# A 4608-token attention and MoE kernel: its first two 256-token chunks in one pass over the weights instead of two

## The chip, the cores and the metric

The kernel runs on one core of a Trainium2 chip. The metric is device time in microseconds of one execution. The engines are named as the profile names them: PE (matmuls; PEld is its weight load), DVE (vector), ACT (activations and copies), POOL (a second, slower vector engine), and SP, which issues most of the DMAs.

## What is computed

The reference computes linear attention with exponential features for 8 batches of 576 tokens and 8 heads of 64, and sends its output, 4608 rows of 512, through a feed-forward layer with a hidden width of 2048. The code calls that layer MoE.

```python
def phi(x):
    proj = np.einsum('bhsd,df->bhsf', x, w_phi)
    proj = proj - np.max(np.abs(proj), axis=-1, keepdims=True)
    return np.concatenate([np.exp(proj), np.exp(-proj)], axis=-1)
q_p, k_p = (phi(q), phi(k))
kv = np.einsum('bhsf,bhsd->bhfd', k_p, v)
z = np.sum(k_p, axis=2)
num = np.einsum('bhsf,bhfd->bhsd', q_p, kv)
den = np.einsum('bhsf,bhf->bhs', q_p, z)[..., None] + 1e-06
attn = num / den                       # then (4608, 512)

h = x @ w_in                           # 512 -> 2048
g = h * (1.0 / (1.0 + np.exp(-1.702 * h)))
out = g @ w_out                        # 2048 -> 512
```

## The kernel before

All matmuls of the bulk run in 16 bits, with each operand split into a high and a low half (`eh` and `el`, `gh` and `gl`, `w16[:, i, 0]` and `w16[:, i, 1]`), so that a product takes three matmuls. The attention of a batch writes its output, already transposed and split, into a tile `x` of which there are three buffers.

The MoE weights come from memory as 64-bit numbers. `load_weights(j, bank)` takes block j (128 of the 2048 hidden columns) of both weight matrices: it loads 512 KB for each, and ACT (`raw<-raw`, `hb<-raw` or `wy<-raw`, the cast to `w`), DVE (two steps on `hb` or `wy`) and DVE or POOL (the low half `w`) make the two halves. For the first 8 blocks the intermediate is a PSUM tile `hb`, for the others an SBUF tile `wy`. There are 16 blocks j, so 32 conversions.

`moe_chunk(sb, c0, n, part_)` does n tokens. For each block j it does 12 matmuls (or more, at a border between batches) into a PSUM tile `hb`, then on ACT and DVE in turn `th` (tanh), `g`, `gh` and `gl`, and then three matmuls for each 128 tokens into an accumulator `ab`. There are three `ab` buffers, so a chunk of 256 tokens holds two of them from its first block to its last, when ACT evicts them into a tile `e` that is stored.

The first 512 tokens go in chunks of 256, all others in chunks of 384. Before the change each of the two chunks of 256 is done twice: with `part_` 0 over j = 0 to 7, with `part_` 1 over j = 8 to 15. After the first pass ACT copies the two accumulators into a tile named `kept`, which takes one of the three `x` buffers; after the second DVE adds the kept row to the accumulator on its way out:

```python
row = kept[:, c0 // P + m] if part_ is not None else None
if part_ == 0:
    R.scalar.activation(row, acc[m], AF.Copy, scale=OS)
    continue
```

Nothing in this kernel is issued in the order of its source. A recorder collects every operation with its tiles, and a planner then puts them in an order for each engine: at each step the operation that can start first by the planner's own costs, and among those that could start now, the one with the lowest place. The places come from a table, `PLACES`, with one pair of numbers for each group of operations (a head pair of attention, the load of a weight block, a chunk), and a group that the table reaches has its pair from there, whatever the source says. Operations that may run on more than one engine (`R.two`, `R.three`, `R.evac`) go where the planner's costs, weighted by the numbers in `price`, put them. Since one line records all of these, the profile shows one line, L467, for nearly everything, and the names of tiles tell the work apart.

Of the kernel before, what the change touches and what calls it, by code (L numbers as in the profile page):

```python
# [8 lines left out]
F32 = mybir.dt.float32  # L9
# [90 lines left out]
class _Op:  # L100
# [5 lines left out]


PLACES = (
# [26 lines left out]
)  # L135
_READY = {"tensor": 215.0, "scalar": 150.0, "vector": 130.0, "gpsimd": 95.0, "sync": 100.0}

# [38 lines left out]


class Recorder:
    price = dict(tensor=1.000, scalar=0.001, vector=2.059, gpsimd=1.247, sync=1.000)

    def __init__(self, nc):
        self.nc, self.ops = nc, []
# [291 lines left out]
def attn_moe_fast(ctx, tc, q, k, v, w_phi, w_in, w_out, out):  # L474
# [4 lines left out]
    NT, DM = out.shape  # L479
# [6 lines left out]
    CH = 384  # L486
# [3 lines left out]
    NH = 2  # L490
# [11 lines left out]
    R = Recorder(nc)  # L502
# [7 lines left out]
    def static(name, shape, dt):  # L510
# [18 lines left out]
        x=([P, 2, NCT, S], F16), th=([P, CH], F32), g=([P, CH], F32), gh=([P, CH], F16),  # L529
# [9 lines left out]
    def new(nm):  # L539
        return R.tile(pools[nm])  # L540
# [117 lines left out]
    def w1(j, part, ct):  # L658
        return w16[:, 2 * j, part, ct * P : (ct + 1) * P]

    def w2(j, part):
        return w16[:, 2 * j + 1, part]
# [452 lines left out]
    def store(sb, col, osb, queue):  # L1115
        p0 = 0
        while p0 < P:
            b, n, row, step = out_rows(col + p0)
            n = min(n, P - p0)
            row += (2 * sb + b) * S  # L1120
            if step == 1:
                dst = out[row : row + n, :]
            else:
                dst = out[row : row + 4 * (n - 1) + 1 : 4, :]
            queue.dma_start(dst, osb[p0 : p0 + n])
            p0 += n
# [3 lines left out]
    def moe_chunk(sb, c0, n, part_=None):  # L1130

        pieces = []
        c = c0
        while c < c0 + n:
            b = c // S
            e = min(c0 + n, (b + 1) * S)
            pieces.append((2 * sb + b, c - b * S, e - b * S, c - c0))
            c = e
        js = range(NJ) if part_ is None else range(part_ * NJ // NH, (part_ + 1) * NJ // NH)
        acc = [R.tile(ab, whole=True) for m in range(n // P)]  # L1140
        for j in js:
            hps = R.tile(hb, whole=True)[:, 0:n]
            for b, a0, a1, o0 in pieces:
                o = hps[:, o0 : o0 + a1 - a0]
                for ct in range(NCT):
                    xh, xl = (t[:, ct, a0:a1] for t in xs[b])
                    last = ct == NCT - 1
                    R.tensor.matmul(o, w1(j, 0, ct), xh, start=ct == 0, stop=False)
                    R.tensor.matmul(o, w1(j, 0, ct), xl, start=False, stop=False)
                    R.tensor.matmul(o, w1(j, 1, ct), xh, start=False, stop=last)  # L1150
            th = new("th")[:, 0:n]
            R.scalar.activation(th, hps, AF.Tanh, scale=0.851 / (XS * WS))
            g = new("g")[:, 0:n]
            R.vector.scalar_tensor_tensor(g, th, 1.0, hps, ALU.add, ALU.mult)
            gh = new("gh")[:, 0:n]
            gl = new("gl")[:, 0:n]
            sc = 0.5 * GS / (XS * WS)
            R.scalar.activation(gh, g, AF.Copy, scale=sc)
            R.vector.scalar_tensor_tensor(gl, g, sc, gh, ALU.mult, ALU.subtract)
            first, last = j == js[0], j == js[-1]  # L1160
            if j == NJ // 2:
                chunks.append(c0)
                i = len(chunks)
                R.vector.tensor_reduce(fin[:, i - 1 : i], g[0:1], AX.X, ALU.add)
            for m in range(n // P):
                s = slice(m * P, (m + 1) * P)
                R.tensor.matmul(acc[m], gh[:, s], w2(j, 0), start=first, stop=False)
                R.tensor.matmul(acc[m], gh[:, s], w2(j, 1), start=False, stop=False)
                R.tensor.matmul(acc[m], gl[:, s], w2(j, 0), start=False, stop=last)
        for m in range(n // P):  # L1170
# [4 lines that stand above are left out]
            end = c0 + n == SB * S and sb == B // SB - 1  # L1175
            osb = new("e")
            if part_ is not None:
                R.vector.scalar_tensor_tensor(osb, acc[m], OS, row, ALU.mult, ALU.add)
            elif end and m:
                R.vector.tensor_scalar(osb, acc[m], OS, None, ALU.mult)  # L1180
            else:
                R.scalar.activation(osb, acc[m], AF.Copy, scale=OS)
            store(sb, c0 + m * P, osb, R.scalar if end and m == 1 else R.sync)
# [82 lines left out]
    for part_ in range(NH):  # L1266
        js = range(part_ * NJ // NH, (part_ + 1) * NJ // NH)
        v0, dv = WV[part_]
# [1 line left out]
            R.part(v0 + dv * i, v0 + dv * (i + 1))  # L1270
            load_weights(j, (lambda: R.tile(hb, whole=True)) if j < NPS else (lambda: new("wy")))
    attention(1)
    kept = new("x").rearrange("p t c s -> p (t c s)").bitcast(F32)
    kept = kept[:, 0 : 4 * DM].rearrange("p (i n) -> p i n", i=4)
    attention(2)

    for part_ in range(NH):
        for c in (0, 256):
            v0 = (512 * part_ + c) / CH / NH
            R.part(v0, v0 + 256 / CH / NH, ("vector", "scalar"))  # L1280
            moe_chunk(0, c, 256, part_)
    for i in range(NBLK):
        R.part(3.0 + 0.2 * i, 3.0 + 0.2 * i, after=250e3)
        weight_max(i)
    for sb in range(B // SB):
        c = 0 if sb else 512
        for n in (CH, CH, CH) if sb else (256, CH):
            v0 = (SB * S * sb + c) / CH
# [189 lines left out]
```

## Time and profile before

| | before |
|---|---|
| median of 3 runs | 1050.89 us (1050.89 to 1051.35) |
| the profiled execution | 1050.94 us, span 1049.5 us |
| PE busy | 1013.7 us, 9914 matmuls |
| DVE busy | 733.7 us |
| ACT busy | 651.6 us |
| POOL busy | 283.2 us |
| HBM read, written | 45.15 MB, 9.44 MB |

The span is from the first to the last instruction. Busy times are summed over an engine's instructions without counting overlaps twice; matmuls are pipelined, so a busy PE may still have room. In 40 slices of 26 us the shares of time look as follows, in tenths (9 is 90% or more); PEclk is the clock granted to PE, in tenths of full speed:

```profile
PE   7869899999999999999999999999999999999997
DVE  5899999999999989999533226776876765323232
ACT  5989899888588878899332235565565554222221
```

The chain of waits that ended last is for 83% of the span PE, for 6% DVE and for 6% ACT.

### The profile page before, as it was taken

To read this page: it belongs to the slowest core of one execution; us is meant where nothing else is said; L and a number is where in the kernel's file an instruction comes from. 1 tells how busy PE (TensorE), PEld (TensorE's weight loads), DVE (VectorE), ACT (ScalarE), POOL (GpSimd) and SP (SyncE) were. 2 spreads that over 40 slices of the span, in tenths; PEclk is the share of its full clock that TensorE was granted. 3 is DMA by queue.
4 is the path that set the end of the run, shared out by engine and by line. 5 is a ranking of instruction groups with operands and counts; after the bars stand their busy time and mean duration, and the time that the engine had idled before them with its cause. 6 is when DMAs were issued, how large, how long until landed. Compare 5 with 4: busy or idle time off the path is not lost.

```text
span 1049.5 us, 24669 instructions
## 1 busy us (share of the span) xinstructions
PE 1013.7 (97%) x9914; PEld 667.6 (64%) x9914; DVE 733.7 (70%) x1465; ACT 651.6 (62%) x1449; POOL 283.2 (27%) x396
## 2 busy tenths in 40 slices
PE   7869899999999999999999999999999999999997
PEld 5646677778666667668664455677755665576543
DVE  5899999999999989999533226776876765323232
ACT  5989899888588878899332235565565554222221
POOL 1225655433334735454200001132211111000000
PEclk8989999999999999999999999999999999999999
DMA  9756655444236453536112011232230120000101
GB/s 239 213 179 152 135 122 149 100 122 99 51 91 98 94 136 72 117 81 124 47 29 42 1 31 49 53 77 47 52 74 20 31 52 11 1 31 1 31 1 33
DMA packets 181019, 80.92 MB, mean 77 GB/s; under 512 B 149536, under 2 KB 174240, under 8 KB 180896
## 3 DMA queue, kind: packets, MB, share of 16 engines
q1 hardware_dynamic: 178048, 78.35, 31.7%
q8 instruction: 79, 1.29, 0.5%
q10 hardware_dynamic: 2848, 0.92, 0.4%
q14 instruction: 44, 0.36, 0.1%
HBM read 45.15 MB, written 9.44 MB: 52 GB/s over the span
## 4 chain that ended last, share of the span: by engine, by line
PE 83%; DVE 6%; ACT 6%; issue 2%; DMA 1%; POOL 0%; SPq 0%; ACTq 0%; DVEq 0%; POOLq 0%
PE ab L467 34%; PE hb L467 32%; PE at L467 17%; ACT e L467 1%; DVE el L467 1%; DVE wy L467 1%; DVE hb L467 1%; ACT x L467 1%; DVE gl L467 1%; ACT eh L467 1%; ACT w L467 1%; DMA tl<-in_v_dram 0%; DMA qt<-in_q_dram 0%; DVE sm L467 0%; DVE t L467 0%
## 5 line engine op out<-in xcount | busy, mean ns | idle before, releaser
L467 PE MATMUL hb<-x,w 128*128 128x192 f16 (+3 forms) x3264 | 448.0, 279 | 1.1 <-DVE g L467 0.6
L467 PEld LDWEIGHTS <-w 128*128 128x128 f16 x3264 | 277.6, 98 | 99.9 <-issue 1.9
L467 PE MATMUL ab<-w,gh 128*128 128x512 f16 x1152 | 340.1, 379 | 0.6 <-ACT gh L467 0.2
L467 ACT ACTIVATE th<-hb 128x384 f32<-128x384 f32 (+1 forms) x208 | 97.1, 467 | 207.4 <-PE hb L467 206.3
L467 DVE SCALAR_TENSOR_TENSOR g<-th,hb 128x384 f32<-128x384 f32 (+1 forms) x208 | 107.9, 519 | 166.8 <-ACT th L467 165.5
L467 PE MATMUL ab<-w,gl 128*128 128x512 f16 x576 | 207.8, 379 | 1.5 <-DVE gl L467 1.4
L467 PEld LDWEIGHTS <-gh 128*128 128x128 f16 x1152 | 101.2, 97 | 96.0 <-ACT gh L467 20.9
L467 DVE SCALAR_TENSOR_TENSOR gl<-g,gh 128x384 f16<-128x384 f32 (+1 forms) x208 | 120.1, 578 | 46.0 <-ACT gh L467 45.2
L467 ACT ACTIVATE gh<-g 128x384 f16<-128x384 f32 (+1 forms) x208 | 103.9, 500 | 67.3 <-DVE g L467 64.7
L467 ACT CAST eh<-e 128x512 f16<-128x512 f32 x212 | 127.9, 624 | 1.2 <-PE at L467 0.6
L467 PEld LDWEIGHTS <-eh 128*128 128x128 f16 x1856 | 111.5, 97 | 26.7 <-ACT eh L467 3.5
L467 DVE TENSOR_TENSOR el<-e,eh 128x512 f16<-128x512 f32 x161 | 116.1, 738 | 15.2 <-ACT eh L467 11.0
L467 POOL TENSOR_TENSOR el<-e,eh 128x512 f16<-128x512 f32 x71 | 86.7, 1224 | 109.3 <-ACT eh L467 76.5
L467 PEld LDWEIGHTS <-gl 128*128 128x128 f16 x576 | 55.0, 97 | 71.4 <-DVE gl L467 31.2
L467 PE MATMUL at<-ph,xT 128*128 128x128 f16 x1024 | 94.9, 220 | 2.0 <-DVE t L467 1.0
L467 PEld LDWEIGHTS <-el 128*128 128x128 f16 x928 | 85.7, 98 | 15.3 <-DVE el L467 4.5
L467 ACT ACTIVATE e<-t 128x512 f32<-128x512 f32 x128 | 76.3, 629 | 20.4 <-DVE t L467 16.9
L467 ACT ACTIVATE e<-at 128x512 f32<-128x512 f32 x136 | 76.9, 602 | 17.7 <-PE at L467 17.1
L467 POOL TENSOR_TENSOR n<-n,cs 128x132 f32<-128x132 f32 (+1 forms) x74 | 42.4, 576 | 159.0 <-ACT n L467 144.5
L467 PEld LDWEIGHTS <-xT 128*128 128x128 f16 x1056 | 73.6, 98 | 15.2 <-issue 2.3
L467 PE MATMUL at<-kz,eh 128*128 128x66 f16 x960 | 78.7, 193 | 1.9 <-DVE x L467 0.7
L467 PE MATMUL at<-vs,eh 128*128 128x66 f16 x896 | 71.0, 194 | 0.0
(184 smaller groups left out, 1288.3 us busy)
## 6 DMA issues: line engine op xcount, KB each, us to landing
kt<-in_k_dram SPq DMA_DIRECT2D x32, 256.0 KB, 3.0
qt<-in_q_dram SPq DMA_DIRECT2D x32, 256.0 KB, 2.9
raw<-in_moe_w_in_dram SPq DMA_DIRECT2D x16, 512.0 KB, 4.0
raw<-in_moe_w_out_dram SPq DMA_DIRECT2D x16, 512.0 KB, 4.4
vn<-in_v_dram SPq DMA_DIRECT2D x62, 128.0 KB, 3.1
out_dram<-e SPq DMA_DIRECT2D x38, 128.0 KB, 2.4
out_dram<-e SPq DMA_DIRECT2D x16, 256.0 KB, 2.7
xT<-xs SPq DMA_TRANSPOSE x68, 2.8
```

The source lines that it names most:

```text
L467: f(*[g(a) for a in o.args], **{k: g(a) for k, a in o.kw.items()})
```

## The change

The two chunks of 256 tokens are each done once, over all 16 weight blocks. The tile `kept` is no longer made, so that the three `x` buffers go round among the scratch tile of the first batch and the batches alone. ACT no longer copies accumulators into it, and DVE no longer adds it; ACT evicts the four accumulators as it does for all other chunks. The operations of `moe_chunk` are otherwise the same. There are two groups fewer, and the table of places and two of the planner's prices are other numbers throughout.

```diff
 PLACES = (
-    (-1000.000, -1000.000), (-319.749, -277.364), (-292.885, 143.728), (-190.514, -96.843), (-328.012, -90.457),
...
+    (-1000.000, -1000.000), (-247.092, -16.724), (-252.980, 213.780), (-303.420, 28.872), (-247.129, -68.214),
...
 class Recorder:
-    price = dict(tensor=1.000, scalar=0.001, vector=2.059, gpsimd=1.247, sync=1.000)
+    price = dict(tensor=1.000, scalar=0.009, vector=2.162, gpsimd=1.253, sync=1.000)
...
     attention(1)
-    kept = new("x").rearrange("p t c s -> p (t c s)").bitcast(F32)
-    kept = kept[:, 0 : 4 * DM].rearrange("p (i n) -> p i n", i=4)
     attention(2)
 
-    for part_ in range(NH):
-        for c in (0, 256):
-            v0 = (512 * part_ + c) / CH / NH
-            R.part(v0, v0 + 256 / CH / NH, ("vector", "scalar"))
-            moe_chunk(0, c, 256, part_)
+    for c in (0, 256):
+        v0 = c / CH
+        R.part(v0, v0 + 256 / CH, ("vector", "scalar"))
+        moe_chunk(0, c, 256)
```

What the new table does shows in the order of the engines. On DVE, just ahead of the first `g` of the MoE (the first block of the first chunk), the order was this; `hb` and `raw` belong to the conversion of weights, `el`, `mq`, `nf` and `x` to attention:

```order
L467 SCALAR_TENSOR_TENSOR hb_67<-hb_67,raw_169 128x512
L467 TENSOR_TENSOR xf_124<-nf_121,rc_160 128x2x2x64
L467 SCALAR_TENSOR_TENSOR hb_68<-raw_171,hb_68 128x512
L467 TENSOR_TENSOR w_248<-hb_67,w_248 128x512
L467 SCALAR_TENSOR_TENSOR hb_68<-hb_68,raw_171 128x512
L467 TENSOR_TENSOR el_98<-e_88,eh_93 128x512
L467 TENSOR_TENSOR el_99<-e_91,eh_94 128x512
L467 TENSOR_TENSOR x_127<-at_66,x_127 128x256
```

With the change the same place reads as follows:

```order
L466 TENSOR_TENSOR w_248<-wy_172,w_248 128x512
L466 SCALAR_TENSOR_TENSOR wy_173<-wy_173,raw_170 128x512
L466 TENSOR_TENSOR x_127<-at_66,x_127 128x256
L466 SCALAR_TENSOR_TENSOR wy_172<-raw_171,wy_172 128x512
L466 TENSOR_SCALAR rc_161<-nf_121 128x4
L466 TENSOR_TENSOR w_248<-wy_173,w_248 128x512
L466 RECIPROCAL rc_161<-rc_161 128x4
L466 TENSOR_TENSOR xf_124<-nf_121,rc_161 128x2x2x64
```

The conversions have moved ahead: before, DVE was still at the blocks that go through `hb`, now it is at those that go through `wy`. 47 conversion steps stand ahead of the first `g` before, 62 with the change.

The second place is the seventeenth `g` on DVE, the first block of the second half of the work of these chunks. Before, it stands among the last conversions:

```order
L467 SCALAR_TENSOR_TENSOR wy_172<-raw_170,wy_172 128x512
L467 TENSOR_TENSOR nf_120<-at_66,n_119 128x198
L467 SCALAR_TENSOR_TENSOR wy_173<-wy_173,raw_169 128x512
L467 TENSOR_TENSOR nf_120<-at_65,n_118 128x198
L467 TENSOR_REDUCE sm_140<-at_66 128x4
L467 SCALAR_TENSOR_TENSOR wy_172<-wy_172,raw_170 128x512
L467 SCALAR_TENSOR_TENSOR g_131<-th_129,hb_68 128x256
```

With the change it stands just behind the last of them:

```order
L466 TENSOR_TENSOR x_127<-at_65,x_127 128x256
L466 TENSOR_TENSOR art_243<-art_243,rc_163 128x8
L466 SCALAR_TENSOR_TENSOR wy_173<-wy_173,raw_169 128x512
L466 TENSOR_TENSOR xo_125<-xf_123,xo_125 128x512
L466 SCALAR_TENSOR_TENSOR g_131<-th_129,hb_67 128x256
L466 SCALAR_TENSOR_TENSOR g_132<-th_130,hb_68 128x256
```

The `wy` step here is the 89th and last conversion step that DVE has; before, 72 of 86 stood ahead of this `g`, and 14 behind it.

The third place is on ACT, where the accumulators leave. Before, ACT copies them into the kept tile (`x_126`) ahead of two tanh steps; with the change the same two accumulators leave only after the sixteenth block, into `e` tiles that are stored:

```order
L467 CAST xo_125<-xf_123 128x512
L467 CAST eh_94<-e_88 128x512
L467 ACTIVATE x_126<-ab_71 128x512
L467 ACTIVATE x_126<-ab_69 128x512
L467 ACTIVATE th_129<-hb_68 128x256
L467 ACTIVATE th_130<-hb_67 128x256
```

```order
L466 CAST eh_95<-e_92 128x512
L466 ACTIVATE e_91<-at_65 128x512
L466 ACTIVATE e_88<-ab_71 128x512
L466 ACTIVATE e_89<-ab_70 128x512
L466 ACTIVATE gh_134<-g_132 128x256
```

The four copies of this kind have gone from ACT, and four additions from DVE.

49 rows, old and new, of the table PLACES are left out of this document.

## The prediction

> **What bounds the kernel now.** I read the page's busy line and its forty slices first, then the window table by stage, then the waits of PE, then the groups of instructions by form.
>
> ```profile
> PE 1013.7 (97%) x9914; PEld 667.6 (64%) x9914; DVE 733.7 (70%) x1465; ACT 651.6 (62%) x1449; POOL 283.2 (27%) x396
> ...
> 0.00:20.00 20.00, 15.61 (x77) 11.88 (x78) 10.53 (x31) 9.23 (x18) 4.27 (x40) 0.83 0.97 257
> 20.00:80.00 60.00, 45.91 (x329) 32.76 (x328) 52.70 (x103) 55.05 (x121) 11.69 (x18) 0.94 0.68 192
> 80.00:150.00 70.00, 64.48 (x772) 47.30 (x768) 67.10 (x135) 64.96 (x153) 43.66 (x52) 0.98 0.64 142
> 150.00:250.00 100.00, 97.84 (x1276) 73.32 (x1277) 93.98 (x196) 86.19 (x204) 44.48 (x55) 1.00 0.47 116
> 250.00:500.00 250.00, 248.88 (x3076) 170.80 (x3074) 234.57 (x470) 208.63 (x474) 119.08 (x153) 1.00 0.45 96
> 500.00:1049.50 549.50, 540.94 (x4398) 331.55 (x4397) 274.80 (x535) 227.58 (x483) 60.03 (x80) 1.00 0.14 34
> ```
>
> The columns of a window are its length, the busy time of PE, PEld, DVE, ACT and POOL, the granted clock, the DMA share and GB/s. PE is idle for 35.8 us of 1049.5, and most of it lies early: 4.4 us up to 20, 14.1 up to 80, 5.5 up to 150, 2.2 up to 250, then 1.1 in 250 us. So from about 150 us on the time is PE's work, nothing else, and a microsecond that PE loses before is not given back. In 80 to 150 us DVE is busy for 96% and ACT for 93%: they must convert weights and make the features of attention before PE has operands. The end is not touched by the change.
>
> ```profile
> 82.47 0.42 DVE L467 SCALAR_TENSOR_TENSOR g<-th,hb 128x256 f32<-128x256 f32 x1
> ...
> 83.04 0.68 DVE L467 SCALAR_TENSOR_TENSOR wy<-raw,wy 128x512 f32<-128x512 f32 x1
> 83.64 0.42 DVE L467 SCALAR_TENSOR_TENSOR gl<-g,gh 128x256 f16<-128x256 f32 x1
> ...
> 157.24 0.77 DVE L467 SCALAR_TENSOR_TENSOR wy<-wy,raw 128x512 int32<-128x512 int32 x1
> 157.93 0.41 DVE L467 SCALAR_TENSOR_TENSOR g<-th,hb 128x256 f32<-128x256 f32 x1
> ```
>
> These are two marks on DVE: the first g of a 256-token block (82.47 us) and the seventeenth (157.93), the first block of the second half of the weights. An instruction shown as 0.68 is followed 0.60 us later by the next, so on a full DVE a duration costs 0.08 less than the row says.
>
> **The change part by part.** (1) Sums between passes. Four ACT copies into the kept tile and four DVE additions go; four plain ACT evictions come.
>
> ```profile
> L467 ACT ACTIVATE x<-ab 128x512 f32<-128x512 f32 x4 | 2.3, 594 | 0.0
> L467 DVE SCALAR_TENSOR_TENSOR e<-ab,x 128x512 f32<-128x512 f32 x4 | 2.7, 686 | 0.0
> ```
>
> ACT is even over the whole program (four go, four come), DVE is relieved of 4 x 0.61 = 2.4 us. The additions stand after 191 us, where PE has no gaps for them to fill: on PE they are worth nothing. PE's matmuls are the same in number and shape.
>
> (2) The order. A block of 256 tokens needs its weights. Two passes give PE 32 blocks in the order 16 blocks over half of the weights, then 16 over the other half; one pass gives 16 blocks over all weights, then 16 again. I counted DVE's rows ahead of the seventeenth g in both orders. Conversion steps (w, wy, hb<-raw): 72 before, 89 now, all that DVE has. Attention steps on 512 columns: 87 before, 80 now. Small attention steps: 77 and 75. MoE steps: 32 and 32.
>
> ```profile
> L467 DVE SCALAR_TENSOR_TENSOR hb<-hb,raw 128x512 int32<-128x512 int32 x16 | 11.0, 693 | 1.1 <-ACT raw L467 1.0
> L467 DVE TENSOR_TENSOR w<-hb,w 128x512 f16<-128x512 f32 x16 | 11.0, 688 | 3.2 <-ACT w L467 3.1
> L467 DVE TENSOR_TENSOR xs<-qt,xs 128x512 f16<-128x512 f32 x18 | 13.1, 728 | 2.7 <-ACT xs L467 2.5 <-POOL xs L467 0.2
> L467 DVE TENSOR_TENSOR nf<-at,n 128x198 f32<-128x198 f32 x56 | 20.0, 356 | 1.5 <-POOL n L467 0.9
> L467 ACT CAST w<-wy 128x512 f16<-128x512 f32 x15 | 9.4, 629 | 2.2 <-DVE wy L467 2.1
> ```
>
> At 0.61 us for a conversion step, 0.62 for a large and 0.28 for a small attention step: 17 x 0.61 - 7 x 0.62 - 2 x 0.28 = +5.5 us of DVE work ahead of the same MoE block. On ACT there are 89 conversion steps for 74, 116 large attention steps for 125, no copies to the kept tile for four, one small step less: with 0.08 off the rows of 629 and 594 ns, and 0.2 for the small one, 15 x 0.55 - 9 x 0.55 - 4 x 0.51 - 0.2 = +1.1 us.
>
> On PE the same 16 blocks stand ahead of the mark, but 62 attention matmuls fewer (875 before, 813 now).
>
> ```profile
> 166.81 1.28 PE at L467 x35
> ```
>
> 35 of them take 1.28 us, 0.037 each, so PE has 2.3 us less to do until it needs that block. If DVE paces this stage, PE waits 5.5 + 2.3 = 7.8 us longer up to the mark; if ACT does, 1.1 + 2.3 = 3.4.
>
> (3) What can absorb it. Conversions need no result of PE, so more of them early can stand in DVE's idle time. DVE is idle for 9.5 us up to 20 us (start, first loads: not to be had), 7.3 in 20 to 80 and 2.9 in 80 to 150. 15 of the 17 extra steps stand ahead of the first g (62 for 47), in the stretch with the 7.3. Bounds: nothing absorbed, +7.8; all 7.3 + 2.9 used, 7.8 - 10.2 = -2.4. Before, 47 conversions already stood in that stretch and left the 7.3 us open, because the conversions themselves go back and forth between ACT and DVE (the row w<-hb above: 3.1 us of waiting for ACT w). I take half of what would come from bringing 20 to 80 us to the idle share of 80 to 150 (2.9 of 70, or 2.5 of 60): (7.3 - 2.5) / 2 = 2.4. So 7.8 - 2.4 = +5.4 us.
>
> (4) The loads. Some five weight blocks more are loaded ahead of the first block; the queue of SP has them earlier, among the k, q and v loads.
>
> ```profile
> raw<-in_moe_w_in_dram SPq DMA_DIRECT2D x16, 512.0 KB, 4.0
> 40.00:50.00 10.00, 8.32 (x56) 6.09 (x55) 8.31 (x16) 9.48 (x21) 0.00 (x0) 1.00 0.86 257
> ```
>
> 5 x 0.5 MB at the 257 GB/s of that window are 10 us; up to 80 us the DMA engines are busy for 0.97 x 20 + 0.68 x 60 = 60 us, so 70 of 80 would be. It fits, and I put nothing; without that cover a conversion waits for its load, 4.0 us from issue to landing.
>
> (5) The place in memory. With the kept tile gone the third x buffer goes to batch 2 without a wait for the second pass, and its attention ends earlier in the order. From 250 us on PE has 1.1 us of gaps in 250, so at most 1.1 us is to be had. Some elementwise steps have moved between DVE and POOL with the new prices; on the whole DVE has 24 steps fewer and POOL 29 more. After 150 us that is hidden behind PE's matmuls; up to 250 us it had 2.2 us of gaps left, and that much it could cost where the cover is thin.
>
> The sum: 1050.9 + 5.4 = 1056.3 us. The profiled execution took 1050.94 us for a span of 1049.5, the median of the runs is 1050.89, so no correction is needed between them.
>
> Is PE really at its limit where it shows 100%?
>
> ```profile
> 951.87 3.90 PE ab L467 x18
> 955.77 3.96 PE hb L467 x48
> ```
>
> 18 matmuls of 512 columns in 3.90 us are 0.217 each, 48 of 192 in 3.96 us 0.083: both 0.42 to 0.43 ns a column, with no room for a wait between them. The Trainium skill (Perfetto Trace Analysis, Identifying the Most-Contended Engine) says that matmul busy time is a poor measure of headroom and LDWEIGHTS busy time a better one; with PEld at 64% it would leave room to win lost time back, and the sum would be anywhere down to no change. The two rows decide against that here.
>
> **The rivals.** (A) The conversions fill DVE's idle time wholly and the stage comes out as it was: for it speaks that 7.3 us are idle in 20 to 80 us, against it that they stayed idle with 47 conversions at hand. At the bound of ACT (+3.4) less the same 2.4 it is +1.0, less 4.8 it is -1.4, in the middle -0.2: 1050.7.
>
> (B) Faster: PE makes up at the thirty-second block what it waits for at the seventeenth, because attention matmuls stand between. The point is the last block of both chunks. Up to it DVE now has 3 conversion steps more, 4 large attention steps and 2 additions fewer, one small step more (3 x 0.61 - 4 x 0.62 - 2 x 0.61 + 0.3 = -1.6 us), ACT four conversions, two large and three small steps and two copies fewer (4 x 0.55 + 2 x 0.55 + 3 x 0.2 + 2 x 0.51, or -4.9 us), PE 32 small matmuls (-1.2 us). That gives -0.4 by DVE and -3.7 by ACT, mean -2.0; with the 1.1 us of gaps beyond 250 us, 1047.8. It decides if PE shows no wait longer than before around the seventeenth block. Against it: PE was gapless from there on, so there is nothing to make up from.
>
> (C) The longer stall costs clock.
>
> ```profile
> 70.00:80.00 10.00, 5.51 (x38) 3.54 (x39) 8.23 (x19) 8.94 (x20) 2.53 (x3) 0.66 0.65 186
> PE ab L467 <- ACT e L467: 3.1, 2, 2.4
> ```
>
> In this window PE was busy for 5.51 us of 10 and the granted clock was 0.66; the longest single wait of PE anywhere in the run was 2.4 us. One more such window at the second chunk, with PE full, would cost (1 - 0.66) x 10 = 3.4 us: 1059.7. The Trainium skill (TensorE: Matmul & The Clock Gate, HAM oscillation) puts the threshold at a gap of some 3.4 us. Here the clock fell with no gap above 2.4, so by the row the risk is larger than by the rule; by the rule, stalls in pieces below it would leave 1056.3.
>
> **How the numbers follow.** The forecast gets 0.42, C 0.17, A 0.2, B 0.21. A measurement of this kernel tells 0.2% from no change, 2.1 us: 1048.8 to 1053.0. Forecast and C are slower but for a small share, which I weigh against A's upper end: slower 0.59, same 0.2, faster 0.21. The likeliest case alone spans 1053 to 1058.7 (+7.8 with nothing absorbed). The range takes in B's centre and C with nothing absorbed (7.8 + 3.4, 1062.1): 1047 to 1062.
>
> **What would show it.** The first hb matmul of the MoE, at 76.7 us before, comes 3 to 8 us later; the seventeenth g, at 157.93, stands at 161 to 164; PE's gaps up to 150 us grow from 24.0 to about 27, with the rest between 150 and 170; after 200 us PE is gapless, and all later marks are late by one and the same amount. I am wrong if the first block is late but the seventeenth isn't (DVE had room), or if the gaps of PE up to 170 us are no longer than before.

## The result, and the profile after

| | before | after |
|---|---|---|
| median | 1051.12 us (4 runs, 1050.89 to 1052.25) | 1065.05 us (4 runs, 1064.02 to 1065.21) |
| ratio | | 1.0129, 95% interval 1.0117 to 1.0142 |
| the profiled execution | 1050.94 us, span 1049.5 us | 1064.9 us, span 1063.1 us |
| mean granted clock | 0.990 | 0.983 |

The change costs 14 us. Forecast were 1056.3 us and a range of 1047 to 1062: the sign was right, the size wrong and outside the range.

The stages of the changed kernel, in the window table with the same columns as in the prediction (length, busy time of PE, PEld, DVE, ACT, POOL, granted clock, DMA share, GB/s):

```profile
0.00:20.00 20.00, 15.40 (x84) 11.96 (x85) 11.77 (x32) 9.70 (x19) 4.37 (x40) 0.91 0.95 262
20.00:80.00 60.00, 44.20 (x289) 30.74 (x288) 51.50 (x93) 51.76 (x113) 10.26 (x15) 0.86 0.70 204
80.00:150.00 70.00, 59.80 (x615) 41.49 (x615) 65.66 (x134) 62.67 (x146) 41.59 (x47) 0.93 0.58 152
150.00:250.00 100.00, 96.70 (x1276) 71.91 (x1277) 84.43 (x181) 79.14 (x188) 42.46 (x54) 1.00 0.38 88
```

Up to 150 us PE is idle for 30.6 us where it was 24.0, and part of what counts as busy ran at a lower clock: 0.86 and 0.93, for 0.94 and 0.98. The other engines are not fuller than before but emptier (DVE 51.50 for 52.70 in 20 to 80 us, ACT 51.76 for 55.05). Two stretches hold the loss, here of the kernel before and then of the change; between them, from 92 to 130 us, PE is idle for 0.9 us where it was 4.8, so a part comes back:

```profile
57.00:92.00 35.00, 25.49 (x227) 17.43 (x226) 32.38 (x74) 32.59 (x78) 14.10 (x24) 0.90 0.56 159
130.00:170.00 40.00, 38.99 (x477) 28.75 (x476) 38.55 (x75) 36.66 (x84) 22.06 (x21) 1.00 0.53 134
```

```profile
57.00:92.00 35.00, 20.82 (x105) 12.80 (x104) 29.00 (x62) 28.37 (x60) 7.18 (x10) 0.61 0.55 170
130.00:170.00 40.00, 32.98 (x393) 22.86 (x391) 37.38 (x74) 35.75 (x83) 22.46 (x27) 1.00 0.56 133
```

In the first stretch PE does 105 matmuls for 227, at a clock of 0.61; in the second it is idle for 7.0 us of 40 instead of 1.0. The two marks on DVE that the prediction used, the first and the seventeenth g (the second row holds two in one):

```profile
93.57 0.42 DVE L466 SCALAR_TENSOR_TENSOR g<-th,hb 128x256 f32<-128x256 f32 x1 [0.50 <-ACT th L466]
...
166.15 0.88 DVE L466 SCALAR_TENSOR_TENSOR g<-th,hb 128x256 f32<-128x256 f32 x2
```

They are 11.1 and 8.2 us late. From the 91st of the 208 blocks on the lag is between 10.0 and 12.7 us (14.5 at a single block), and 12.1 at the end. What PE does in the first stretch, in the timeline of PE (start, duration, tiles and shapes, count, and in brackets how long PE was idle before and for whom), only the rows with a wait of 0.9 us or more:

```profile
59.36 0.27 PE L466 MATMUL at<-kz,eqth 128*128 128x132 f16 x1 [1.91 <-DVE kz L466]
61.96 0.40 PE L466 MATMUL at<-kz,eqth 128*128 128x132 f16 x2 [1.89 <-DVE nt L466]
64.73 0.66 PE L466 MATMUL at<-ident,xf 128*128 128x128 f32 x2 [1.92 <-DVE nt L466]
66.31 1.12 PE L466 MATMUL at<-ident,t 128*128 128x128 f32 x4 [0.92 <-DVE x L466]
69.63 2.82 PE L466 MATMUL at<-x,kf 128*66 128x256 f32 x6 [2.20 <-ACT x L466]
...
81.79 0.29 PE L466 MATMUL at<-ii,zt 128*128 128x64 f16 x4 [1.41 <-ACT zt L466]
85.57 0.69 PE L466 MATMUL at<-ident,xf 128*128 128x128 f32 x2 [2.39 <-POOL xf L466]
```

These rows are attention of the first batch. `ident,t`, `x,kf` and `ident,xf` belong to its exact queries (the 256 tokens that the first chunk needs, computed on 32-bit operands), with one group of eight `x,kf` for each of the four head pairs; `kz,eqth` belongs to its last tokens. Each step feeds ACT and DVE and waits for what they send back. Up to 57 us PE has done the same matmuls in both kernels, within one of each kind, but for four `x,kf` that are missing now. What differs is the order in which the rest stands in PE's list. Three rows of the kernel before, and then of the change one group and the ACT step that makes its operand `x`:

```profile
55.46 0.65 PE L467 MATMUL at<-x,kf 128*66 128x256 f32 x2 [0.85 <-ACT kf L467]
...
60.74 1.89 PE L467 MATMUL at<-x,kf 128*66 128x256 f32 x8
...
66.44 0.62 PE L467 MATMUL at<-x,kf 128*66 128x256 f32 x2 [1.07 <-DVE nt L467]
```

```profile
73.78 2.63 PE L466 MATMUL at<-x,kf 128*66 128x256 f32 x8
```

```profile
55.66 1.08 ACT L466 ACTIVATE x<-at 128x512 f32<-128x512 f32 x2
```

Before, the four groups of `x,kf` start at 48.62, 55.46, 60.74 and 66.44 us, with steps of other head pairs between them. Now they start at 47.71, 69.63, 73.78 and 77.15: three of them stand behind all the waits of the rows above. By the buffers that the program names, the group at 73.78 reads the `x` that ACT had ready at 56.74 us, so it had its operands for 17 us and stood behind other steps. The change is hardly late when it enters this stretch; its list gives PE nothing else to do ahead of these waits. The 105 matmuls for 227 are mostly what follows from that: 147 of the 227 run after 77.2 us, when the kernel before was past its last `x,kf` and the change had just come to them.

Of the 13.6 us between the spans, 12.1 stand ahead of the end of the last DVE step (the evictions of the last chunk, before and after):

```profile
1041.16 1.34 DVE L467 TENSOR_SCALAR e<-ab 128x512 f32<-128x512 f32 x2 [0.97 <-PE ab L467]
```

```profile
1053.23 1.34 DVE L466 TENSOR_SCALAR e<-ab 128x512 f32<-128x512 f32 x2 [0.97 <-PE ab L466]
```

From there to the end of the span it is 7.0 us before and 8.5 after, 1.5 us that no step of the program explains; the section on the hardware comes back to it.

### The profile page after: what moved, and what is told of

It reads as the page before. It is cut to its first block, busy times and chain, and to the rows that moved or that the text cites. A ratio compares the mean times of both kernels' runs of the same rounds, so it can differ in the third digit from the quotient of the medians.

```text
span 1063.1 us, 24696 instructions
## 1 busy us (share of the span) xinstructions
PE 1016.6 (96%) x9914; PEld 667.7 (63%) x9914; DVE 733.1 (69%) x1441; ACT 647.5 (61%) x1440; POOL 303.0 (29%) x425
## 4 chain that ended last, share of the span: by engine, by line
PE 80%; DVE 8%; ACT 6%; issue 3%; DMA 1%; POOL 0%; ACTq 0%; SPq 0%; DVEq 0%; POOLq 0%
PE ab L466 33%; PE hb L466 31%; PE at L466 17%; ACT e L466 2%; DVE el L466 1%; ACT eh L466 1%; DVE t L466 1%; ACT x L466 1%; DVE sm L466 1%; DVE wy L466 1%; DVE hb L466 1%; DVE gl L466 1%; DVE w L466 0%; DVE g L466 0%; DMA x<-xo 0%
## 5 line engine op out<-in xcount | busy, mean ns | idle before, releaser
L466 DVE SCALAR_TENSOR_TENSOR gl<-g,gh 128x384 f16<-128x384 f32 (+1 forms) x208 | 114.3, 551 | 47.9 <-ACT gh L466 47.5
L466 DVE TENSOR_TENSOR el<-e,eh 128x512 f16<-128x512 f32 x166 | 124.7, 767 | 20.6 <-ACT eh L466 12.3
L466 ACT CAST eh<-e 128x512 f16<-128x512 f32 x209 | 125.5, 625 | 4.7 <-PE at L466 4.4
L466 POOL TENSOR_TENSOR el<-e,eh 128x512 f16<-128x512 f32 x66 | 78.9, 1197 | 83.3 <-ACT eh L466 66.9
L466 POOL TENSOR_TENSOR n<-n,cs 128x132 f32<-128x132 f32 (+1 forms) x89 | 53.4, 602 | 153.4 <-ACT n L466 106.8
L466 ACT ACTIVATE e<-at 128x512 f32<-128x512 f32 x136 | 76.6, 603 | 13.5 <-PE at L466 13.2
L466 PE MATMUL at<-kz,eh 128*128 128x66 f16 x960 | 75.9, 193 | 2.3 <-DVE nt L466 1.3
```

Source lines behind the costliest of these rows:

```text
L466: f(*[g(a) for a in o.args], **{k: g(a) for k, a in o.kw.items()})
```

## The experiments

Unless said otherwise an experiment keeps the planned order and alters what is issued from it, so that no other step moves. Where the totals are closer than their intervals (about 1.5 us either way), the marks decide: the first g (93.57 us after, 82.47 before) and the seventeenth (166.15 and 157.93). A mark is read from one profiled execution.

### The numbers without the one pass

```diff
 # the kernel before (two passes, kept tile), with
-PLACES, price   of before
+PLACES, price   of the change (the two chunk entries cut into four)
```

> Two passes as before, with the sums kept between them, but with the changed kernel's table of places and prices. Order theory (the new numbers put conversions ahead of attention, and that costs; one pass or two does not matter): about 1065 us, within 2 of the changed kernel. Structure theory (a chunk that runs through all 32 weight blocks at once needs the second half of the conversions sooner, whatever the numbers): 1049 to 1054 us, as the kernel before. Between 1054 and 1062 both have a part.

Measured: 1080.68 us, ratio 1.0276 (1.0254 to 1.0298). Worse than either kernel, so neither bracket holds. Its window table:

```profile
57.00:92.00 35.00, 20.02 (x100) 12.33 (x101) 29.07 (x62) 28.44 (x60) 6.99 (x10) 0.63 0.55 170
130.00:170.00 40.00, 31.84 (x346) 24.13 (x347) 34.24 (x65) 35.13 (x77) 19.01 (x24) 0.70 0.48 121
```

The first row is that of the changed kernel almost to the digit, and the first g stands at 94.47. So **the first stretch comes with the numbers, not with the single pass**: two passes under these numbers stall there just as long. What follows is another matter. The ninth block, in two passes the first of the second chunk of tokens, comes at 156.8 us (126.7 before): these numbers put the second half of the first batch's queries late, which one pass needs only at its seventeenth block. There is no reverse, one pass with the numbers of before: with them the planner comes to a point from which no step can start.

### More and less work on DVE

```diff
 # kernel before, nine of the steps wy|hb <- max(c * raw, same) of 40 to 150 us
+repeat the step
```

> The kernel before in its own order, with 9 of the conversion steps wy<-raw,wy on DVE between 40 and 150 us done twice (same result). That is 9 x 0.60 = 5.4 us of DVE work, the excess that the prediction worked out for the change. Work theory: the seventeenth g comes 5 us later or more and the total is 1056 to 1060; if the wait also costs clock, up to 1064. Absorption theory (DVE has 7.3 + 2.9 us of idle time up to 150 us to take it): under +2, 1051 to 1053.

Measured: 1058.44 us, ratio 1.0068 (1.0052 to 1.0085); the seventeenth g at 166.33. 5.4 us of DVE work cost 7.2. The absorption theory falls, and for this kernel the work theory's range holds.

```diff
 # changed kernel, nine of the same steps
-the step
```

> The changed kernel in its own order, with 9 of the conversion steps wy<-raw,wy on DVE between 40 and 150 us left out (the weights of those blocks then come out otherwise where they are negative; PE's work is the same): 5.4 us of DVE work less. Work theory: 1065 - 5.4 = 1059.6 or lower, down to 1054 if the clock comes back with it. If the wait for a weight load at 140 us or ACT sets the end: no less than 1063.

Measured: 1065.98 us, ratio 1.0136; the seventeenth g at 166.0, the first at 93.4. Nothing. So work added to the kernel before costs more than itself, and work taken from the changed kernel gives nothing: the changed kernel's stage isn't paced by how much DVE has to do. Neither test was made on the other kernel.

### Holding the clock

```diff
 # changed kernel, ahead of twelve waiting PE steps o
+for _ in range(n): matmul(o.out[:, 0:128], ones, ones)
```

> The changed kernel in its own order; ahead of twelve PE steps between about 54 and 90 us, where PE waits 0.9 to 2.4 us each, matmuls of 128 columns on the tile of ones are added (209 in all), so that PE is busy while it waits. They write where the next real matmul starts afresh. Clock theory (the granted clock of 0.50 from 60 to 75 and 84 to 90 us stretches the chain of waits itself): clock above 0.9 there, the first g 3 to 6 us earlier than 93.6, total 1058 to 1062. Work theory (DVE sets when PE's operands come, whatever PE's clock): the clock rises, the marks stay within 1 us, total 1064 to 1066.

Measured: 1069.27 us, above both brackets; the clock rose to 0.94 in 20 to 80 us and 1.00 in 80 to 150, and the marks came 4.7 to 5.1 us later. The added matmuls (256 of them, by the trace) did not fill the waits, they queued behind them (the timeline of PE in this kernel):

```profile
58.03 1.50 PE L476 MATMUL at<-ones 128*128 128x128 f16 x24 [1.60 <-ACT x L480]
...
63.20 0.96 PE L476 MATMUL at<-ones 128*128 128x66 f16 x26 [2.05 <-DVE nt L480]
```

They need no operand, so what they waited for was the bank of PSUM that they write to, until ACT or DVE had emptied it. That made two new questions, with four kernels.

```diff
-w = o.out[:, 0:128]
+w = ab.aps[1][:, 0:128]      # a bank that holds nothing between 54 and 88 us
```

> The changed kernel in its own order, and ahead of the same PE steps that wait between 54 and 90 us matmuls of 128 columns on the ones tile again, fewer of them, now into an ab bank that is idle, so that they don't wait for a bank themselves. Clock theory: clock above 0.9 from 60 to 90 us, x,kf x8 in 1.9 us instead of 3.68, the first g 2 to 4 us earlier than 93.6, total 1061 to 1063. If the chain runs through DVE and ACT: clock up, marks within 1 us, 1064 to 1066.

Measured: 1063.20 us, ratio 1.0117 (1.0100 to 1.0133).

```profile
57.00:92.00 35.00, 29.50 (x371) 24.14 (x371) 32.14 (x67) 31.47 (x68) 7.41 (x11) 1.00 0.59 180
```

The clock is 1.00 throughout, eight `x,kf` take 1.9 us, the first g comes at 91.38 and the seventeenth at 163.7. So the clock is worth 2.2 us at the first mark and 2.5 at the second. It is an effect of the stall that makes it a little longer, not its cause.

### Banks and load buffers

```diff
-at tiles started at 54 to 88 us: slots at0..at2
+the same tiles: slots at0..at2, ab0..ab2 (the one longest free)
```

> The changed kernel in its own order; 17 of the at tiles that PE starts between about 54 and 88 us are spread over the three at and the three ab banks of PSUM instead of the three at banks alone (no ab tile lives there then). Bank theory (PE's waits for ACT x and DVE nt at 58 to 75 us, 1.6 to 2.2 us each, are waits for a bank to be emptied, as the added matmuls that waited just as long showed): the waits shrink by half or more, the first g 3 us earlier than 93.6 or more, total 1059 to 1062. If what empties the bank is also what makes the operand: marks within 1 us, 1064 to 1066.

Measured: 1064.65 us. The first g comes at 91.54, but the seventeenth at 166.2 as ever. The timeline of PE in this kernel:

```profile
60.41 0.27 PE L486 MATMUL at<-kz,eqth 128*128 128x132 f16 x1 [3.15 <-DVE kz L486]
67.73 1.12 PE L486 MATMUL at<-x,kf 128*66 128x256 f32 x2 [4.40 <-ACT x L486]
```

With more banks PE hardly waits less (it is idle for 13.5 us from 57 to 92 us, for 14.2), it waits in fewer and longer pieces, now for operands. The banks were the first thing that was missing, the operands the next.

```diff
-raw: 3 buffers
+raw: 5 buffers up to 150 us (two in the third x buffer, idle until then)
```

> The changed kernel in its own order; from the seventh weight load on until about 150 us, five raw buffers take turns instead of three (the two more lie in the third x buffer, which nothing else uses by then). Load theory (a conversion waits for its load because the buffer came free late: 4.49 us at 139.84 in the changed kernel, 3.83 at 59.0 with less DVE work): the seventeenth g 4 us earlier than 166.2 or more, total 1059 to 1061. If the loads are hidden: marks within 1 us, 1064 to 1066.

Measured: 1064.32 us; the first g 0.6 us earlier, the seventeenth 1.4. The load of 4.49 us in the second stretch was in the chain of waits, and with it gone the next wait took its place.

> The spread banks and the five raw buffers together. Bank and load theory: both gains, 1054 to 1058. If only one of them holds, its own gain alone; if neither, 1064 to 1066.

Measured: 1063.47 us, the seventeenth g at 162.6: together 3.6 us at the mark, 1.6 in the total.

> The changed kernel in its own order with the clock held through an idle bank and with five raw buffers, both as in the runs that had one of them. If the gains on the lag of the last blocks (2.0 and 2.1 us) add up: 1060.5 to 1062. If they are the same microseconds: 1062.5 to 1064.

Measured: 1062.65 us, ratio 1.0109 (1.0092 to 1.0126), by the total just in the bracket for gains that are the same microseconds. At the seventeenth g, 162.4, they nearly add up (3.7 us for 2.5 and 1.4), and a part is lost again later: the last of the 208 g is 2.7 us earlier, for 2.1 with either alone.

> The kernel before in its own order with the same two additions (matmuls on the ones tile into an idle bank where PE waits between 55 and 79 us, five raw buffers until 115 us). If its dip to a clock of 0.5 at 72 to 78 us costs it as the longer dip costs the changed kernel, about a third of that: 1049.5 to 1051. If its stall is not PE's clock: 1051 to 1052.

Measured: 1053.00 us, ratio 1.0015 (1.0005 to 1.0025). With the clock at 1.00 in 57 to 92 us for 0.90, and the raw buffers added, the kernel before gains nothing and pays a little. No version run here beats it.

### Another order of the same steps

```diff
+list the first 3600 steps anew: engines, buffers, order of DMAs as planned;
+of two ready steps on an engine the one with the lower rank goes first
-rank = planner's
+rank = place in the old list                          (j1)
+rank = the same, first batch's exact part 150 lower   (i3)
+rank = the same + shifts per group, searched          (i1; i2 from two passes)
```

> The changed kernel with the same steps, engines, buffers and order of loads, but the first 3600 steps listed anew: numbers per group of steps (attention of a head pair, a weight block, a chunk) shift which of two ready steps goes first on an engine, searched for PE ending its part of them early. Order theory (one pass costs nothing of its own, its list was poor): PE's lag of 12 us goes wholly, 1051 to 1054. Structure theory (all conversions have to be done by the sixteenth block instead of the thirty-second, so that DVE and ACT set the pace whatever the list): a part of it goes, 1056 to 1062.

> The kernel before with its first 3600 steps listed anew in the same way, with the same search. If its list was as far from the best as that of the changed kernel, it gains as much as the run above, and one pass stays behind it by 8 us or more (structure theory): 1043 to 1049. If only the list of the changed kernel was poor (order theory): 1049 to 1052.

> The changed kernel with the first batch's loads, keys and exact queries (what the first chunk of tokens needs) 150 places earlier in the list, ahead of weight conversions; all else kept. Order theory: the first g 5 us earlier than 93.6 or more, and the total with it: 1058 to 1061. Structure theory: the first g that much earlier, but the conversions that were passed are missed at blocks 9 to 16, the seventeenth g within 2 us of 166.2, total 1063 to 1066.

> The control to the three relisted kernels: the changed kernel's first 3600 steps go through the same new listing, with no step preferred (the place in the old list decides between two ready steps). If listing anew costs nothing by itself: 1064 to 1066, and bringing the exact attention forward cost 11 us. If most of the loss came from it: 1070 to 1076.

Measured: i1 1074.59, i2 1067.65, i3 1076.42, j1 1077.35 us (ratios 1.0222, 1.0160, 1.0242, 1.0253). The control spoils the set: listing anew, with nothing preferred, costs 12 us by itself; that the new listing's estimate of when a step can start is coarser than the planner's is a likely reason, not a tested one. Against the control the searched order is 2.8 us better, and the exact part brought forward 0.9, which is within the scatter of the runs. Its marks say more. The late groups of `x,kf` start at 62.09, 65.99 and 68.87 us, in the control at 70.76, 74.91 and 77.95, and PE is idle for 9.8 us from 57 to 92 us instead of 15.1. The first g comes at 86.8, 8.7 us ahead of the control's 95.4. So **the place of the first batch's exact part in the list moves the first block**, with the same steps, engines and buffers. The seventeenth stands at 172.1 for 173.5: all but 1.4 us of what the first block wins is gone by then. i2 has no control and shows nothing. What the four do show is how much hangs on the list: the same steps on the same engines with the same buffers, and 12 us between two orders.

### Is it the conversions at all?

These kernels leave decoding steps out of the changed kernel, more from one to the next.

```diff
 # weight blocks chosen by the time of their decoding
-raw <- scale(raw)              (ACT, some on POOL)
-y   <- max(c * raw, y)         (DVE; not in i4)
-y   <- (y << 3) | raw          (DVE)
```

> The changed kernel in its own order, with the low half of nine weight blocks between 40 and 150 us not decoded (the ACT step raw<-raw and the DVE step wy<-wy,raw of the same block are left out, so these weights come out wrong; PE's work is the same): 9 x 0.56 = 5.0 us less on ACT and 9 x 0.61 = 5.5 us less on DVE. Structure theory (both engines pace the stage together, which is why 5.4 us less on DVE alone gave nothing): 1057 to 1061. If the chain of round trips between engines sets it, not their work: 1063 to 1066.

> The changed kernel in its own order, with the decoding of eight weight blocks between 35 and 62 us left out (16 DVE steps wy or hb<-raw, 7 ACT and 1 POOL steps raw<-raw; those weights come out wrong, PE's work is the same): 16 x 0.60 = 9.6 us less on DVE and 7 x 0.56 = 3.9 us less on ACT, about the 15 conversion steps that stand ahead of the first g in excess of the kernel before. Queue theory (the exact attention stands behind these conversions): first g 6 us earlier than 93.6 or more, total 1056 to 1060. If loads or the round trips between the engines set the front stage: first g within 2 us, total 1063 to 1066.

> The changed kernel in its own order, with all decoding of the 16 weight blocks converted between 35 and 92 us left out (32 DVE steps on hb or wy with raw, 13 ACT and 3 POOL steps raw<-raw; wrong weights, same work for PE): 32 x 0.60 = 19.2 us less on DVE and 13 x 0.56 = 7.3 us less on ACT, twice the excess of conversion work ahead of the first g. Work theory: the first g 8 us or more earlier than 93.6 (85 or less), total 1053 to 1057. Chain theory (round trips of the exact attention between PE, ACT and DVE in the listed order, at half the clock): the first g 2 to 5 us earlier, total 1060 to 1063.

> The same with all decoding between 35 and 170 us left out: 27 weight blocks, 54 DVE steps (32.4 us), 23 ACT steps (12.9 us) and 4 POOL steps. Work theory: the second stall at 140 to 170 us goes too, total 1051 or less. Chain theory: 1056 to 1061.

| left out, DVE and ACT | total | first g | seventeenth g |
|---|---|---|---|
| nothing | 1065.05 us | 93.57 | 166.15 |
| i4: 5.5 and 5.0 us, 40 to 150 us | 1063.54 | 92.8 | 165.3 |
| j4: 9.6 and 3.9 us, 35 to 62 us | 1062.50 | 92.1 | 163.8 |
| k1: 19.2 and 7.3 us, 35 to 92 us | 1063.57 | 89.8 | 163.3 |
| k2: 32.4 and 12.9 us, 35 to 170 us | 1060.86 | 91.1 | 163.2 |

The work and queue theories fall. With 45 us of work gone from the two engines, 4.2 us come back (ratio to the kernel before 1.0090, 1.0073 to 1.0106). The window table and the waits of PE in the last of these kernels:

```profile
60.00:70.00 10.00, 4.16 (x17) 2.65 (x17) 3.61 (x8) 6.11 (x13) 0.41 (x1) 0.54 0.64 208
```

```profile
60.79 0.38 PE L482 MATMUL at<-kz,eqth 128*128 128x132 f16 x2 [1.83 <-DVE nt L482]
63.54 0.66 PE L482 MATMUL at<-ident,xf 128*128 128x128 f32 x2 [1.92 <-DVE nt L482]
65.12 1.12 PE L482 MATMUL at<-ident,t 128*128 128x128 f32 x4 [0.92 <-DVE x L482]
68.44 3.68 PE L482 MATMUL at<-x,kf 128*66 128x256 f32 x8 [2.21 <-ACT x L482]
```

DVE is busy for 3.6 us of 10, and PE waits 1.83, 1.92, 0.92 and 2.21 us at the places where the full changed kernel waits 1.89, 1.92, 0.92 and 2.20. These are round trips (a result is sent to another engine and waited for), not queues (the other engine is still busy with earlier steps). The chain of waits of the changed kernel shows one of them, engine by engine ("issue" is time in which nothing visible was waited for):

```profile
64.73 0.67 PE at L466 x2
65.43 0.38 ACT x L466
65.83 0.44 DVE x L466
66.31 1.13 PE at L466 x4
67.49 0.47 issue
67.96 0.62 ACT hb L466
68.58 0.20 ACT w L466
68.77 0.20 issue
68.97 0.61 ACT x L466
69.63 3.68 PE at L466 x8
```

Every step is short and follows the one before almost at once. (Ahead of it, from 49.85 to 61.92 us, the chain stands on DVE, with decoding steps in it; without them the `kz,eqth` of 61.96 us comes at 60.79.) From 64.73 to 69.63 PE computes for 1.8 us of 4.9, because the list gives it nothing else there, while the group of 73.78 us lies ready. Two ACT conversion steps stand inside (`hb` and `w`, 0.8 us here); these were not among the steps left out, and the low halves on DVE neither, so the last row of the table bounds the decoding, not all of the conversion.

The second stretch stays too. In the last of these kernels, k2, PE is busy for 33.12 us of the 40 from 130 to 170, with DVE busy for 29.95 only:

```profile
130.00:170.00 40.00, 33.12 (x371) 22.54 (x368) 29.95 (x59) 33.45 (x77) 18.07 (x27) 1.00 0.50 139
```

## Why the prediction was wrong

**Step (2), the order, is where it failed.** It counted how much DVE has to do ahead of the seventeenth block, 17 conversion steps more, and let that amount pace the stage. The runs say that the amount does not pace the changed kernel: less of it gives next to nothing (0 for 5.4, 4.2 for 32.4 on DVE and 12.9 on ACT), though more of it costs the kernel before 7.2 us for 5.4. That both go together can be understood, without being shown: the lists are fixed for each engine, and in a fixed list a delay is handed on while an early finish only waits for the next dependent step. The unabsorbed figure of that step, +7.8 us at the seventeenth block, is close to the measured 8.2, but taking the counted work away moves this mark by 3.0 us at the most: the agreement is chance.

What sets the loss in the first stretch was in the order and was not looked for: where the exact queries of the first batch stand in PE's list. PE does nearly the same up to 57 us; then the second group of `x,kf` comes at 69.63 us where it came at 55.46, with PE waiting in between. That the numbers and not the single pass bring this stretch is shown by two passes under the same numbers (second group at 70.64). That the place in the list moves the first block, by 8.7 us, is shown by the relisted kernel with the exact part earlier, against its control. That the total would follow is not shown: there 0.9 us came back.

**Step (3), the absorption of 2.4 us, did not happen** in the kernel before: nine repeated steps cost it 7.2 us although DVE is idle for 7.3 + 2.9 us up to 150. That idle time took up nothing. The change, too, came out above the figure with nothing absorbed.

**Step (4), the loads at nothing,** was off by 0.6 to 1.4 us at the marks, and 4.49 us of one load stood in the chain of waits; the fallback price of 4.0 us for a wait was near that, but removing the wait did not give its length back. **Steps (1) and (5)**, at nothing and at 1.1 us at most, were not tested by themselves; nothing in the marks speaks for a gain from either.

**Rival (C), the clock,** was a rival where it should have been a term. It was put at the second chunk, at 3.4 us. It came at the first, deeper and longer than a window of 0.66, and its price is 2.2 to 2.5 us at the marks. The changed kernel in windows of 3 us:

```profile
60.00:63.00 3.00, 0.92 (x9) 0.68 (x7) 2.74 (x6) 2.11 (x5) 0.41 (x1) 0.50 0.89 330
63.00:66.00 3.00, 0.66 (x2) 0.29 (x2) 2.73 (x6) 2.43 (x6) 0.41 (x1) 0.50 0.58 175
66.00:69.00 3.00, 1.12 (x4) 0.72 (x4) 1.94 (x4) 2.39 (x6) 0.00 (x0) 0.50 0.65 189
...
72.00:75.00 3.00, 3.00 (x10) 1.51 (x9) 1.49 (x4) 1.70 (x6) 0.29 (x1) 0.50 0.69 227
75.00:78.00 3.00, 2.96 (x20) 1.88 (x19) 2.16 (x7) 2.54 (x7) 0.00 (x0) 0.97 0.51 144
```

**Rivals (A) and (B)** are out: nothing was absorbed, and the thirty-second g is 9.6 us late (213.2 and 222.8). Of the signs to look for, the first hb matmul was a bad mark. It came 3.6 us earlier (73.10 for 76.73) while the first g came 11.1 later: the block's matmuls start as soon as one head pair of `x` is there and end with the last. PE's idle time up to 150 us grew by 6.6 us and not 3. That the lag stays the same once PE has no gaps held, only from a later point: the first 90 blocks lie between 4 us early and 13.5 us late, since the two kernels have different attention behind them at the same block.

**What adds up and what stays open.** Of 13.6 us between the spans, 1.5 lie behind the last step. Of the other 12.1, at the last g, holding the clock gives back 2.1 and five raw buffers 2.1, and both together 2.7. Some 9 us remain. None of the clock, the banks, the loads and the decoding, each taken by itself, gives back more than 3.8 there, and for the first stretch the loss is shown to come with the numbers; that the round trips in the listed order make it is read from the traces, and no run here filled those waits with other useful work.

Why PE loses 6 us more in 130 to 170 us was not separated. Neither the load that stood in its chain nor the decoding there is the cause by itself. In the changed kernel the chain of waits stands on ACT from 144.4 to 159.1 us, and the window table has ACT busy for 14.69 us of these 14.70:

```profile
144.40:159.10 14.70, 12.42 (x159) 8.89 (x159) 13.65 (x27) 14.69 (x33) 9.02 (x11) 1.00 0.55 119
```

That is a queue, unlike the round trips of the first stretch. In k2 the chain passes between ACT, DVE and PE in short pieces there, and PE is idle for the same 6.9 us of the 40; but its load is still in the chain (4.50 us), and its other ACT steps are still there. Whether some other list would give one pass the time of before, or a better one, stays open; the relisted kernels can't tell, because listing anew cost more than what was looked for.

## What to carry to other kernels

When a change comes with a new order, don't price it by the work that now stands ahead of a mark. Take the stretch in which the bounding engine waits, list that engine's steps there before and after, in their order, and see whether its waits are queues (the engine that it waits for is full) or round trips (it isn't): a queue is priced by durations, a round trip by what else the list offers meanwhile. And try the price in both directions, adding and taking away, before believing that an engine paces a stage, and do both on the same kernel. Here adding cost the kernel before 7 us, and taking away gave the changed one none.

## What the runs showed of the hardware

**The clock falls without a long gap.** In the changed kernel no wait of PE in the whole run is longer than 2.9 us, and none between 54 and 92 us longer than 2.4; still the granted clock is 0.50 from 60 to 75 us, with PE busy for 0.66 to 1.12 of each 3 us up to 69 (the windows above). The longest wait stands in this row of PE's waits (sum, times, longest):

```profile
PE ab L466 <- ACT e L466: 3.6, 2, 2.9
```

The Trainium skill (TensorE: Matmul & The Clock Gate, HAM oscillation) puts the rule at idle gaps of more than about 3.4 us; by that rule alone the clock would have stayed up here. The measurement decides: waits of 0.9 to 2.2 us with 0.66 to 1.12 us of matmuls in 3 were enough here, and with these waits filled by matmuls into an idle bank the clock stayed at 1.00.

**The end of the program has two lengths.** From the last DVE step to the end of the span it took 6.8 to 7.0 us in four of the profiled kernels and 8.1 to 8.7 in the other sixteen, and the queue that moves instructions carried 6 packets in that time in each of the four and 7 in each of the sixteen. The end of the kernel before (from 1042.5 us) and of the change (from 1054.57):

```profile
q14 instruction: 6, 0.05, 2.3%
```

```profile
q14 instruction: 7, 0.06, 2.1%
```

The four are the kernel before, the two made from it in its own order and its relisted form; the same code with the new numbers is among the sixteen. So 1.5 us of the 14 come from where the program's instructions happen to end, it seems; that the additional packet makes the time is argued from this agreement, and was not tested.
